# A decode block with cached attention: four load slots in the place of a used-up weight, a q projection on column tiles, and a new load order

## The chip, the core and the metric

The kernel runs on one core of a Trainium2 chip. The metric is the device time of one execution in microseconds (us); the median over several executions counts. The engines are PE (matrix products and weight loads), DVE (vector work), ACT (activations), POOL and SP; SP issues all loads here, in one fixed order.

## The reference

Two layers, each of attention over a cache and a gated FFN, for four batches of one new token. Both layers use the same weights and the same caches.

```python
def _A_ref(x, k_cache, v_cache, wq, wo):      # x [4,1,512], caches [4,8,8192,128]
    q = (x @ wq).reshape(B, Sq, 32, 128).transpose(0, 2, 1, 3)
    k = jnp.repeat(k_cache, 4, axis=1); v = jnp.repeat(v_cache, 4, axis=1)
    p = softmax(einsum("bhqd,bhkd->bhqk", q, k) * 128 ** -0.5)
    o = einsum("bhqk,bhkd->bhqd", p, v)
    return o.transpose(0, 2, 1, 3).reshape(B, Sq, 4096) @ wo
def _B_ref(x, w_gate, w_up, w_down):          # F = 1792
    return (silu(x @ w_gate) * (x @ w_up)) @ w_down
x = x + _A_ref(_layernorm(x), ...);  x = x + _B_ref(_layernorm(x), ...)   # twice
```

All is bfloat16. Each cache holds 67 MB, and the four batches are independent of each other.

## The kernel before

**Units.** The caches are read in units of 1 MB: one batch b, one KV head g (8 of them), and one half cp of the 8192 positions. That makes 16 K units and 16 V units for each batch and layer. SBUF has a pool of `NSLOT = 11` slots of 8 KB per partition for them; a unit takes a slot from its load until PE has used it.

**A layer of one batch.** Each K unit is transposed on DVE (L568, two halves) and multiplied with the spread-out q on PE (L580), into four PSUM banks. After 16 units comes a softmax (L598 to L670). Then each V unit is multiplied with the probabilities on PE: as a rule by `rows` (L720, 16 products of 256 columns on four column tiles per unit, after which DVE transposes, adds and scales, L739 to L743), and for the last three groups (`NLATE = 3`) by `columns` (L705, 32 products of four columns). A group is the two V units of one head; its sum stays in one PSUM bank from its first unit to its last. Three banks (4, 5, 6) are shared by all such sums, by the FFN, the q projection and the softmax's transposes. The output projection (L683) follows each group.

**The chain.** When the last layer-0 group of a batch is projected, `chain` runs: add to x, layer norm, FFN (gate and up L758, down L811), layer norm, and the q projection of layer 1 for all heads in two halves (`q_proj`, L460: 64 products of 128x128 weights with four columns in each half), then scale (L523), spread (L473) and copy into `qpad` (L533). Only then can the K units of layer 1 for this batch be multiplied. The stages of K units run in the order `KSEQ`: (layer 0, batch 0), (0,1), (1,0), (0,2), (1,1), (0,3), (1,2), (1,3).

**The order.** `ORDER` is one string of tokens, the order in which SP issues loads: `K` is the next K unit, `a` a V unit of layer 0 (a + batch, head, half), `b` a V unit of layer 1 that is loaded again, `c` a V unit of layer 1 that is not loaded again, because its slot was kept from layer 0, and the weights by name. A `c` token loads nothing; its place only gives a priority. The class `Plan` simulates engines, slots, banks and loads with fixed costs, and from that fixes every engine's order of work, each unit's slot and each sum's bank. At run time semaphores hold the dependencies (waits at L62, loads issued at L92), but the order on an engine does not change. `wq_sb` is 32 KB per partition, and its last use is the q projection of batch 3.

Of the kernel before, what the change touches and what calls it, by code (L numbers as in the profile page):

```python
# [102 lines left out]
class Step:  # L103
    __slots__ = ("eng", "us", "deps", "fn", "prio", "take", "free", "start", "end", "loads", "slot_of", "n")

    def __init__(self, eng, us, fn, deps, prio, take=None, free=None, n=0):
        self.n = n
        self.eng, self.us, self.fn, self.prio = eng, us, fn, prio
        self.deps = [d for d in deps if d is not None]
        self.take, self.free = take, free  # L110
        self.start = self.end = None
        self.slot_of = None


class Plan:
# [3 lines left out]
    PAGE_N = 256  # L119
    LOAD_LEAD = 1.8  # L120
    LOAD_TAIL = 1.7
# [19 lines left out]
    def run(self):  # L141
# [66 lines left out]
        while left:  # L208
# [37 lines left out]
            if s.slot_of is not None:  # L246
                slots.append((s.end + self.HOP, self.slot[s.slot_of]))
            left -= 1
            finish(s)
# [4 lines left out]
    def emit(self):  # L254
        for s in sorted(self.steps + self.loads, key=lambda s: (s.start, s.prio[0])):
            s.fn()


ORDER = ("K c241 c230 K x a061 c201 c021 c310 c240 K c110 c100 c101 c311 a021 K wq K c000 c020 wo3 c001 K K K "
         "K K c231 a060 c040 K c161 c160 K c330 K K c111 c041 K K a071 c301 K a041 K c200 wo0 a070 a050 a040 "  # L260
         "K K K K a010 a020 a051 a031 K c300 K K K a011 K K K wo1 K c331 K wu1 K a000 a001 a030 wo2 wg0 wg1 "
         "wd0 wu0 wd1 a140 a141 a130 a120 a131 K K K K K K K K K K K K K K K K K a121 a150 K a151 a170 K a160 "
         "K K K a161 K K K K K a110 a111 a171 K K a100 a101 b060 K K b061 K b010 b011 b030 b071 b031 b050 "
         "b070 b051 K K K K a250 K K K K K K K a210 K a251 K K K K K a211 a260 a270 K a271 a200 K K a240 K "
         "a231 a201 K K K K a220 a221 a230 K K K a241 K K K a261 b130 b131 K b120 b121 b140 b141 b171 b170 "
         "b150 b151 K a361 a360 K a370 K K K K K K K K a371 K K K K K K a320 a351 a350 a321 a340 a330 a310 "
         "a331 a300 a341 a311 a301 b271 K b270 b260 b210 b211 K b261 K K K K K K K K K K K K K K b221 b250 "
         "b220 b321 b251 b340 b341 b370 b371 b320 b350 b351 b360 b361 ")
NSLOT = 11
NP = 2  # L270
NQB = 1
NLATE = 3


def bass_interleave_layers__gqa_block_cached__swiglu_ffn__decode_kernel(
# [33 lines left out]
    with ExitStack() as es:  # L309
# [57 lines left out]
        prog = {n: sem(f"prog_{n}") for n in engines}  # L367
        sem_slot = [sem(f"sem_slot{i}") for i in range(NSLOT)]
        sem_x = sem("sem_x")
# [85 lines left out]
        def q_proj(heads, deps, tag):  # L455
            def mm():
                bk = pbk(tag)
                for h in heads:
                    for kt in range(KT):
                        op("pe", lambda e: e.matmul(ps[:, bk * BW + h * B:bk * BW + (h + 1) * B],  # L460
                                                    lhsT=wq_sb[:, kt, h * Dh:(h + 1) * Dh],
                                                    rhs=xnT[:, kt * B:(kt + 1) * B],
                                                    start=(kt == 0), stop=(kt == KT - 1)),
                           reads=["wq", "xnT"], writes=[f"pb{bk}"], sig=(kt == KT - 1 and h == heads[-1]))
            return PL.add("pe", 0.029 * KT * len(heads), mm, deps, CHAIN, take=tag, n=2 * KT * len(heads))

        def q_spread(src, n, key, deps, tag):
# [48 lines left out]
        def q_half(b, hf, mm_tag, deps, prior):  # L516
            nh = Hq // 2
            k = kpos[(1, b)] % NQB

            def scl():  # L520
                bk = pbk(mm_tag)
                src = ps[:, bass.ds(bk * BW + b + hf * nh * B, nh, step=B)]
                op("dve", lambda e: e.tensor_scalar(qT2[:, hf * nh:(hf + 1) * nh], src, qscale[:, b:b + 1], None,  # L523
                                                    op0=ALU.mult),
                   reads=[f"pb{bk}", "qscale"], writes=[f"qT2_{hf}"])
            s1 = PL.add("dve", 0.21, scl, deps, CHAIN, free=mm_tag)
            tag = f"qs{b}_{hf}"
            sp = q_spread(qT2[:, hf * nh:(hf + 1) * nh], nh, f"qT2_{hf}", [s1], tag)

            def cp():  # L530
                bk = pbk(tag)
                got = ps[:, bk * BW:bk * BW + NES * nh].rearrange("p (s g j) -> p s g j", s=NES, j=REP)
                op("dve", lambda e: e.tensor_copy(q_diag(k, hf * G // 2, G // 2), got),  # L533
                   reads=[f"pb{bk}"], writes=[f"qpad{k}_{hf}"])
            return PL.add("dve", 0.21, cp, [sp, prior], CHAIN, free=tag)
# [3 lines left out]
        def unit_ap(u, h):  # L539
            s = PL.slot[home[u]]  # L540
            return pool[:, s, h * UE:(h + 1) * UE], f"slot{s}_{h}"

        def load_pair(u):
            kind, l, b, g, cp = u

            def fn():
                s = PL.slot[home[u]]
                cache = A_k_cache if kind == "k" else A_v_cache
                src = cache[b, g, cp * 2 * CR:(cp + 1) * 2 * CR, :].rearrange("(p t) d -> p (t d)", p=P)
                T.dma("sp", pool[:, s, :], src, sem_slot[s], writes=[f"slot{s}_0", f"slot{s}_1"])  # L550
            home[u] = u
            return PL.load(2.515, fn, u)

# [6 lines left out]
        def k_pair(u, ld, prio, prev):  # L560
            _, l, b, g, cp = u
            qbuf = kpos[(l, b)] % NQB
            tr = []
            for h in range(2):
                def t(h=h):
# [6 lines left out]
            def qk():  # L572
                kt = [unit_ap(u, h) for h in range(2)]
                ap = [k[0].rearrange("p (t e j s) -> p t e j s", e=2, j=32, s=2) for k in kt]
                for es_ in range(NES):
                    for a in range(4):
                        rows = slice(32 * a, 32 * (a + 1))
                        for h in range(2):
# [3 lines left out]
                                                        rhs=ap[h][rows, :, es_ // 2, :, es_ % 2],  # L582
                                                        start=(g == 0 and es_ == 0),
                                                        stop=(g == G - 1 and es_ == NES - 1),
                                                        tile_position=(32 * a, 32 * c), skip_group_check=True),
                               reads=[f"qpad{qbuf}_{2 * g // G}", kt[h][1]], writes=[f"pb{a}"],
                               sig=(es_ == NES - 1 and a == 3 and h == 1))
            st = PL.add("pe", 1.95, qk, tr + [qd, prev] + (scores_free[0] or []), prio, n=64)
            st.slot_of = u
            return st  # L590
# [100 lines left out]
        def v_group(l, b, g, lds, prios):  # L691
# [4 lines left out]
            for i, cp in enumerate(VCP):  # L696
                u = ("v", l, b, g, cp)

                def columns(u=u, i=i, cp=cp):
                    bk = pbk(tag)  # L700
                    for h in range(2):
                        ap, key = unit_ap(u, h)
                        for t in range(NB):
# [5 lines left out]
                                                        stop=(i == NCP - 1 and h == 1 and t == NB - 1)),  # L709
                               reads=pt(q) + [key], writes=[f"pb{bk}"], sig=(h == 1 and t == NB - 1))  # L710

                def rows(u=u, i=i, cp=cp):
                    bk = pbk(tag)
                    for h in range(2):
                        ap, key = unit_ap(u, h)
                        v = ap.rearrange("p (t d) -> p t d", d=Dh)
                        for f in range(2):
                            col = p_col(2 * cp + h, g, 8 * f)
                            for n in range(4):
# [6 lines left out]
                                   reads=pt(q) + [key], writes=[f"pb{bk}"], sig=(h == 1 and f == 1 and n == 3))  # L726
                st = PL.add("pe", 1.0 if direct else 0.95, columns if direct else rows,
                            [prev, p_ready[(l, b)], lds.get(u)], prios[i], take=tag if i == 0 else None,
# [5 lines left out]
            def nm():  # L734
                bk = pbk(tag)
                got = ps[:, bk * BW:bk * BW + REP]
                if not direct:
# [7 lines left out]
                   reads=[f"pb{bk}", f"invL{q}", "osum"], writes=[f"oT{l}_{g}"])  # L745
            n = PL.add("dve", 0.17 if direct else 0.6, nm, [prev, inv_ready[(l, b)]], CHAIN, free=tag)
            if l == 0 or b == B - 1:
# [84 lines left out]
        def chain(b, deps, prior):  # L832
# [7 lines left out]
            for hf in range(2):  # L840
                tag = f"q{b}_{hf}"
                mm = q_proj(range(hf * Hq // 2, (hf + 1) * Hq // 2), [cen, mm], tag)
                out_.append(q_half(b, hf, tag, [mm, qs], prior))
            q_ready[(1, b)] = out_

        def w_piece(t_sb, src, key, us):
            return PL.load(us, lambda: T.dma("sp", t_sb, src, sem(f"sem_{key}"), writes=[key]), None)

# [11 lines left out]

        kseq = [("k", l, b, g, cp) for l, b in KSEQ for cp in range(NCP) for g in range(G)]
        VCP = list(range(NCP))
        tokens = ORDER.split()
        kept = {("v", 0) + tuple(int(x) for x in t[1:]) for t in tokens if t[0] == "c"}
        vgroups = [(l, b, g) for b in range(B) for l in range(2) for g in range(G)]
        late_groups = []
        for t in reversed(tokens):
            if t[0] == "b" and len(late_groups) < NLATE and (1, int(t[1]), int(t[2])) not in late_groups:
                late_groups.append((1, int(t[1]), int(t[2])))

# [5 lines left out]
        for npos, t in enumerate(tokens):  # L876
            if t == "K":
                u = kseq[ki]
                ki += 1
                loads[u] = load_pair(u)  # L880
                prio[u] = [npos]
            elif t[0] in "abc":
                u = ("v", int(t[0] != "a")) + tuple(int(x) for x in t[1:])
# [39 lines left out]
        def make_k(i):  # L923
# [6 lines left out]
            for n, u in enumerate(us_):  # L930
                st = k_pair(u, loads[u], prio[u], st)
            last_q[i] = st
# [42 lines left out]
        def fin2():  # L975
            bk = pbk("out")
            op("dve", lambda e: e.tensor_copy(xlast, bank_bf(bk)[0:B * NQ, 0:P]), reads=[f"pb{bk}"], writes=["xrow"])
        PL.add("dve", 0.15, fin2, [s], CHAIN, free="out")

# [36 lines left out]
```

## Time and profile before

| | |
|---|---|
| median of 3 runs | 642.69 us (642.42 to 643.32) |
| the profiled execution | 643.24 us, its span 641.5 us |
| moved on the load queue | 257.19 MB in 41048 packets |
| PE, DVE, ACT busy | 418.5, 421.6, 40.2 us |
| mean granted PE clock | 0.685 |
| K units, V units loaded | 128, 104 |
| median from issue to landing, K and V units | 9.6 and 10.7 us |

The span runs from the first to the last instruction. In the page's second part the span is cut into 40 equal slices of 16 us: PEclk is the PE clock granted in tenths of full speed (9 is 90% or more), DMA the mean busy share of the 16 DMA engines, GB/s what they moved. In the timeline a line is start, duration, engine, line of the kernel, operation, result and operands, shapes, and how many instructions were merged; in square brackets stands how long the engine was idle before it, and what ended that. "issue" there means that the engine waited for nothing that the profile shows. The chain of waits goes back from the last instruction to what released it, step by step, and is read in order of time.

### The profile page before, as it was taken

Reading aid. Unit: us, or ns where it says so; the run is one execution under the profiler, and the core shown is the slowest. Engines: PE = TensorE matmul, PEld = TensorE weight load, DVE = VectorE, ACT = ScalarE, POOL = GpSimd, SP = SyncE. Lnnn points to the kernel's source line nnn. Section 1 sums busy time; section 2 is a strip of 40 time slices with the busy share of each in tenths; the row PEclk is TensorE's granted clock in tenths of the full one; section 3 lists DMA queues with packets and bytes.
Section 4 is the critical chain, followed back from the end, with each engine's and each line's share of the span. In section 5 each row is a group of like instructions: output and inputs, shape, how many; then the busy total and the mean of one; then the engine's idle time right before and its main releaser. Section 6 shows DMA issues by size and latency. Waiting matters only on the chain.

```text
span 641.5 us, 18860 instructions
## 1 busy us (share of the span) xinstructions
PE 418.5 (65%) x8721; PEld 210.1 (33%) x8721; DVE 421.6 (66%) x740; ACT 40.2 (6%) x106; POOL 1.8 (0%) x8
## 2 busy tenths in 40 slices
PE   0276455656677676578775675777666776876765
PEld 0231131215532242235322242224522254622355
DVE  5278864745289979565686976576487763599722
ACT  1000200003000100000200100000200020000200
POOL 1000000000000000000000000000000000000000
PEclk9995676776576789766577686565676675578675
DMA  8999999999999999999999999999999999999991
GB/s 359 411 417 420 407 419 421 406 413 382 403 369 419 421 420 419 420 420 398 415 411 421 420 417 421 420 412 421 404 403 421 418 422 419 393 398 422 420 418 68
DMA packets 41127, 258.39 MB, mean 403 GB/s; under 512 B 3924, under 2 KB 9816, under 8 KB 10840
## 3 DMA queue, kind: packets, MB, share of 16 engines
q1 hardware_dynamic: 41048, 257.19, 97.8%
q8 instruction: 68, 1.11, 0.7%
q14 instruction: 11, 0.09, 0.0%
HBM read 257.17 MB, written 0.00 MB: 401 GB/s over the span
## 4 chain that ended last, share of the span: by engine, by line
DMA 60%; PE 18%; DVE 15%; SPq 4%; issue 2%; ACT 1%
DMA pool<-in_A_k_cache_dram 34%; DMA pool<-in_A_v_cache_dram 26%; DVE pool L568 8%; PE ps L580 7%; PE ps L720 5%; SPq L92 4%; DVE negm L598 2%; PE ps L460 1%; DVE ps L739 1%; PE ps L758 1%; DVE pp L627 1%; PE ps L638 1%; PE ps L683 1%; PE ps L811 1%; DVE osum L741 1%
## 5 line engine op out<-in xcount | busy, mean ns | idle before, releaser
L568 DVE STREAM_TRANSPOSE pool<-pool 128x1024 uint32<-128x1024 uint32 x256 | 303.4, 1223 | 69.0 <-DMA pool<-in_A_k_cache_dram 62.2
L580 PE MATMUL ps<-pool,qpad 32*32 32x512 bf16 x4096 | 229.4, 528 | 84.6 <-DVE pool L568 82.0
L580 PEld LDWEIGHTS ps<-pool,qpad 32*32 32x32 bf16 x4096 | 67.3, 107 | 220.6 <-DVE pool L568 155.0
L720 PE MATMUL ps<-pool,pp 128*32 128x256 bf16 x1952 | 98.2, 352 | 60.5 <-DMA pool<-in_A_v_cache_dram 47.3
L720 PEld LDWEIGHTS ps<-pool,pp 128*32 128x32 bf16 x1952 | 54.6, 116 | 100.5 <-DMA pool<-in_A_v_cache_dram 67.9
L739 DVE STREAM_TRANSPOSE ps<-ps 128x256 f32<-128x256 f32 x61 | 27.9, 457 | 68.9 <-PE ps L720 68.9
L602 ACT ACTIVATE pp<-ps,negm 128x512 bf16<-128x512 f32 x32 | 21.6, 685 | 336.4 <-DVE negm L598 249.2
L683 PE MATMUL ps<-oT,wo_sb 128*128 128x4 bf16 x640 | 22.8, 166 | 15.4 <-DVE oT L743 10.9
L460 PE MATMUL ps<-xnT,wq_sb 128*128 128x4 bf16 x640 | 18.4, 166 | 19.2 <-DMA wq_sb<-in_A_wq_dram 17.5
L683 PEld LDWEIGHTS ps<-oT,wo_sb 128*128 128x128 bf16 x640 | 20.2, 102 | 28.9 <-DVE oT L743 19.1
L598 DVE TENSOR_REDUCE negm<-ps 128x1 f32<-128x512 f32 x32 | 19.8, 679 | 13.0 <-PE ps L580 13.0
L460 PEld LDWEIGHTS ps<-xnT,wq_sb 128*128 128x128 bf16 x640 | 17.6, 103 | 21.0 <-DMA wq_sb<-in_A_wq_dram 17.6
L638 PE MATMUL ps<-ident,pp 128*128 128x128 bf16 x128 | 14.9, 293 | 9.5 <-DVE pp L627 8.8
L638 PEld LDWEIGHTS ps<-ident,pp 128*128 128x128 bf16 x128 | 11.9, 137 | 14.9 <-DVE pp L627 10.8
L446 ACT ACTIVATE lnv<-var,eps_sb 128x4 f32<-128x4 f32 x10 | 3.0, 297 | 219.3 <-DVE var L441 219.3
L741 DVE TENSOR_REDUCE osum<-ps 128x4 f32<-128x32 f32 x61 | 11.7, 191 | 2.1
L743 DVE TENSOR_TENSOR oT<-osum,invL 128x4 bf16<-128x4 f32 x61 | 10.3, 169 | 2.1
L705 PE MATMUL ps<-pp,pool 128*128 128x4 bf16 x192 | 5.9, 167 | 6.5 <-DMA pool<-in_A_v_cache_dram 6.5
L647 ACT ACTIVATE pp<-ps 128x1024 bf16<-128x1024 bf16 x8 | 8.2, 1024 | 23.9 <-PE ps L638 23.9
L627 DVE TENSOR_SCALAR pp<-pp,alpha 128x512 bf16<-128x512 bf16 x32 | 9.0, 343 | 1.1 <-ACT alpha L620 1.1
L758 PE MATMUL ps<-xnT,wg_sb 128*128 128x4 bf16 x280 | 8.2, 166 | 2.1 <-DVE xnT L435 1.5
L811 PE MATMUL ps<-hT,wd_sb 128*128 128x4 bf16 x280 | 8.5, 166 | 1.1 <-DVE hT L803 0.6
(61 smaller groups left out, 126.7 us busy)
## 6 DMA issues: line engine op xcount, KB each, us to landing
pool<-in_A_k_cache_dram SPq DMA_DIRECT2D x128, 1024.0 KB, 9.6
pool<-in_A_v_cache_dram SPq DMA_DIRECT2D x104, 1024.0 KB, 10.7
wq_sb<-in_A_wq_dram SPq DMA_DIRECT2D x1, 4096.0 KB, 24.0
wo_sb<-in_A_wo_dram SPq DMA_DIRECT2D x4, 1024.0 KB, 18.0
wu_sb<-in_B_w_up_dram SPq DMA_DIRECT2D x2, 896.0 KB, 13.9
wg_sb<-in_B_w_gate_dram SPq DMA_DIRECT2D x2, 896.0 KB, 15.9
wd_sb<-in_B_w_down_dram SPq DMA_DIRECT2D x2, 896.0 KB, 12.4
pp<-in_A_x_dram SPq DMA_DIRECT2D x1, 4.0 KB
```

Of the source, the lines that this page charges most:

```text
L92: ins = self.eng[engname].dma_start(out_ap, in_ap)
L460: op("pe", lambda e: e.matmul(ps[:, bk * BW + h * B:bk * BW + (h + 1) * B], lhsT=wq_sb[:, kt, h * Dh:(h + 1) * Dh], rhs=xnT[:, kt * B:(kt ...
L568: op("dve", lambda e: e.transpose(v, v), reads=[key], writes=[key])
L580: op("pe", lambda e: e.matmul(ps[32 * c:32 * (c + 1), a * BW:(a + 1) * BW], lhsT=qpad[rows, qbuf, es_, g, :], rhs=ap[h][rows, :, es_ // 2, ...
L598: op("dve", lambda e: e.tensor_reduce(negm[:, q, a:a + 1], bank(a), AX.X, ALU.max, negate=True), reads=[f"pb{a}"], writes=[f"negm{q}_{a}"])
L602: op("act", lambda e: e.activation(pblk(q)[:, :, a, :], bank(a).rearrange("p (t j) -> p t j", j=32), ACTF.Exp, bias=negm[:, q, a:a + 1], s ...
L627: op("dve", lambda e: e.tensor_scalar(seg, seg, alpha[:, q, a:a + 1], None, op0=ALU.mult), reads=[f"pp{q}_{a}", f"alpha{q}"], writes=[f"pp ...
L638: op("pe", lambda e: e.matmul(stg[:, t * P:(t + 1) * P], lhsT=pp[:, q, blk * P:(blk + 1) * P], rhs=ident[:], is_transpose=True, start=True ...
L683: op("pe", lambda e: e.matmul(ps[:, OPJ * BW + nq * B:OPJ * BW + (nq + 1) * B], lhsT=wo_sb[:, h, nq * P:(nq + 1) * P], rhs=oT[:, l, h, :], ...
L720: op("pe", lambda e: e.matmul(ps[32 * n:32 * (n + 1), bk * BW:bk * BW + 256], lhsT=pp[:, q, col:col + 32], rhs=v[:, 8 * f:8 * (f + 1), 32 ...
L739: op("dve", lambda e: e.transpose(blk, blk), reads=[f"pb{bk}"], writes=[f"pb{bk}"])
L741: op("dve", lambda e: e.tensor_reduce(osum[:], diag, AX.X, ALU.add), reads=[f"pb{bk}"], writes=["osum"])
```

## The change

- Four more slots: the place of `wq_sb` is divided into four slots, handed to the plan when PE has done the last q projection (`gives`). `load_pair` and `unit_ap` go through `slot_sb`.
- The q projection of layer 1 (`q_rows`) holds x on PE and streams wq: 16 products of 512 columns on four column tiles for each half, followed by a transpose of a whole bank on DVE. The first q projection (`q_first`) stays as it was.
- Group 6 of the last batch alone is multiplied by columns (`LATE`), not three groups. The very last V unit comes in two loads of half its size, and its products are split alike (`TAILSPLIT`).
- K units: layer 0 takes heads 4 to 7 ahead of heads 0 to 3, layer 1 the other way round; before, both went by half of the positions and then by head. Code to keep K units too is there, but off (`KM` is 0).
- A new `ORDER`, and new costs in the plan. Of `c` tokens there are 25 in place of 24, of `b` tokens 39 in place of 40; batch 3 keeps seven units where each batch kept six.

```diff
-    LOAD_LEAD = 1.8
+    LOAD_LEAD = 2.1
...
+            for i in range(s.gives):
+                slots.append((s.end + self.HOP, self.nslots + i))
...
-         "wd0 wu0 wd1 a140 a141 a130 a120 a131 K K K K K K K K K K K K K K K K K a121 a150 K a151 a170 K a160 "
...
-         "a331 a300 a341 a311 a301 b271 K b270 b260 b210 b211 K b261 K K K K K K K K K K K K K K b221 b250 "
-         "b220 b321 b251 b340 b341 b370 b371 b320 b350 b351 b360 b361 ")
+ORDER = ("c320 K c321 c041 c240 a061 wg0 K a071 c241 wo2 K x wq K c201 a051 a021 K c131 K c130 a031 c311 K K "
+         "c110 K c111 K K c120 c121 c051 c040 K K K K K wo0 K a020 K a030 wg1 K a060 wo3 K c261 a070 K c050 K "
+         "K K K c301 c260 K K K K K K a050 K a040 a041 a000 a001 wo1 a011 a010 c340 wd1 wu0 c341 wu1 wd0 a140 "
+         "a141 a160 a171 a170 a161 K K K K K c200 K K K K K K c300 K K K K K a100 a101 a150 a151 K K a130 K "
+         "a120 a121 K K K K K a111 K K K K K a110 K K a131 b000 b001 K b021 b030 b020 b070 b031 b071 b010 "
+         "b011 K K K a210 K K K K K K K K K K K K K a270 a271 K a220 a250 a221 K a211 K K a230 a240 K K K "
+         "b100 c060 K a200 a241 K c061 K a251 a231 K K K K a260 a201 a261 b150 K K b101 b161 b151 b170 b160 "
+         "b171 b140 b141 K a310 a350 K K K K K K K K K K a351 K K K K K a370 a361 a360 a371 a330 a301 a340 "
+         "a320 a341 a311 a300 a331 a321 b210 b211 b270 b271 b230 K K K K K K K K K K K K K K K K b221 b251 "
+         "b250 b220 b371 b370 b351 b310 b360 b231 b350 b330 b331 b361 ")
 NSLOT = 11
-NLATE = 3
+LATE = (6, )
+KM = (0, 0, 0, 0)
+TAILSPLIT = True
...
+        def q_rows(hf, deps, tag):
+            nh = Hq // 2
+            def mm():
+                bk = pbk(tag)
+                for kt in range(KT):
+                    w = wq_sb[:, kt, hf * nh * Dh:(hf + 1) * nh * Dh].rearrange("p (h d) -> p h d", d=Dh)
+                    for n in range(4):
+                        op("pe", lambda e: e.matmul(ps[32 * n:32 * n + B, bk * BW:(bk + 1) * BW],
+                                                    lhsT=xnT[:, kt * B:(kt + 1) * B],
+                                                    rhs=w[:, :, 32 * n:32 * (n + 1)],
+                                                    start=(kt == 0), stop=(kt == KT - 1), tile_position=(0, 32 * n)),
...
+                blk = bank(bk).bitcast(mybir.dt.uint32)
+                op("dve", lambda e: e.transpose(blk, blk), reads=[f"pb{bk}"], writes=[f"pb{bk}"])
+                src = ps[:, bass.ds(bk * BW + b, nh, step=32)]
...
-            s1 = PL.add("dve", 0.21, scl, deps, CHAIN, free=mm_tag)
+            s1 = PL.add("dve", 0.98, scl, deps, CHAIN, free=mm_tag)
...
+        def slot_sb(s):
+            return pool[:, s, :] if s < NSLOT else wq_sb[:, s - NSLOT, :]
...
-            return PL.load(2.515, fn, u)
+            if u != last_unit:
+                return PL.load(2.495, fn, u)
+            def half(h):
+                s = PL.slot[home[u]]
+                src = A_v_cache[b, g, cp * 2 * CR:(cp + 1) * 2 * CR, :].rearrange("(p h t) d -> p h (t d)", p=P, h=2)
+                T.dma("sp", slot_sb(s)[:, h * UE:(h + 1) * UE], src[:, h, :], sem_half if h == 0 else sem_slot[s],
...
+            return [PL.load(1.25, lambda: half(0), u), PL.load(1.25, lambda: half(1), None)]
...
+                if u == last_unit:
+                    lds[u], first = lds[u][1], lds[u][0]
+                    prev = PL.add("pe", 0.5, lambda columns=columns: columns(hs=(0,)),
+                                  [prev, p_ready[(l, b)], first], prios[i], take=tag if i == 0 else None, n=32)
+                    st = PL.add("pe", 0.5, lambda columns=columns: columns(hs=(1,)), [prev, lds[u]], prios[i], n=32)
...
-                st = PL.add("pe", 1.0 if direct else 0.95, columns if direct else rows,
+                st = PL.add("pe", 1.0 if direct else 1.02, columns if direct else rows,
...
-            n = PL.add("dve", 0.17 if direct else 0.6, nm, [prev, inv_ready[(l, b)]], CHAIN, free=tag)
+            n = PL.add("dve", 0.17 if direct else 0.88, nm, [prev, inv_ready[(l, b)]], CHAIN, free=tag)
...
-                mm = q_proj(range(hf * Hq // 2, (hf + 1) * Hq // 2), [cen, mm], tag)
+                mm = q_rows(hf, [cen, mm], tag)
                 out_.append(q_half(b, hf, tag, [mm, qs], prior))
+            if b == B - 1:
+                mm.gives = KT
...
-        kseq = [("k", l, b, g, cp) for l, b in KSEQ for cp in range(NCP) for g in range(G)]
+        k_order = [(g, cp) for cp in range(NCP) for g in range(G)]
+        k_order = [x for x in k_order if x[0] >= G // 2] + [x for x in k_order if x[0] < G // 2]
+        def k_units(l, b):
+            stay = k_order[len(k_order) - KM[b]:]
+            seq = k_order if l == 0 else stay + [x for x in k_order[len(k_order) // 2:] if x not in stay] + \
+                k_order[:len(k_order) // 2]
+            return [("k", l, b) + x for x in seq]
+        kseq = [u for l, b in KSEQ for u in k_units(l, b)]
...
-        late_groups = []
-        for t in reversed(tokens):
...
+        late_groups = [(1, B - 1, g) for g in LATE]
```

## The prediction

> **What bounds the kernel now.** I read the slices of the page first, then its DMA queues, then windows of four microseconds where the GB/s row sags, then the timeline inside the worst of them, then the end of the chain of waits.
>
> ```profile
> PEclk9995676776576789766577686565676675578675
> DMA  8999999999999999999999999999999999999991
> GB/s 359 411 417 420 407 419 421 406 413 382 403 369 419 421 420 419 420 420 398 415 411 421 420 417 421 420 412 421 404 403 421 418 422 419 393 398 422 420 418 68
> q1 hardware_dynamic: 41048, 257.19, 97.8%
> ```
>
> The DMA row is full from the second slice to the last but one, and the rate is flat at 420 to 421 GB/s wherever only 1 MB cache units move. 257.19 MB at 420.5 GB/s are 611.6 us of the 641.5 us span: this is a stream, and work on an engine counts only where it stops the stream or stands after it. The other 30 us are a head of about 2.75 us, a tail of about 13 us after the stream, and some 14 us of sag. Part of the sag is weight pieces in short packets (DMA share above 1.0 at a lower rate), which both kernels load alike. The rest is a stream that ran dry:
>
> ```profile
> 168.00:172.00 4.00, 2.97 (x84) 2.81 (x85) 1.49 (x9) 0.50 (x2) 0.00 (x0) 0.50 1.01 422
> 172.00:176.00 4.00, 2.29 (x83) 2.02 (x84) 0.46 (x2) 0.00 (x0) 0.00 (x0) 0.50 0.91 369
> 176.00:180.00 4.00, 2.63 (x57) 1.64 (x60) 2.72 (x6) 0.00 (x0) 0.00 (x0) 0.50 0.52 178
> 544.00:548.00 4.00, 3.91 (x111) 3.25 (x108) 3.21 (x11) 0.25 (x1) 0.00 (x0) 0.50 0.96 385
> 548.00:552.00 4.00, 3.55 (x72) 2.36 (x68) 1.23 (x8) 0.17 (x1) 0.00 (x0) 0.50 0.93 367
> 552.00:556.00 4.00, 3.96 (x123) 3.37 (x120) 1.23 (x5) 0.33 (x2) 0.00 (x0) 0.50 1.01 397
> ```
>
> The last three columns are granted clock, DMA share, GB/s. Against 421, 172 to 180 us lost 4 x (52 + 243) / 421 = 2.8 us (2.3 us by the share) and 544 to 556 us lost 4 x (36 + 54 + 24) / 421 = 1.1 us. Both lie under a serial chain (last output projection, FFN, layer norm, q projection) that must end before the next 16 K units can be used, while the slots fill with them. Batch 0's chain in the timeline:
>
> ```profile
> 169.74 1.86 PE L460 MATMUL ps<-xnT,wq_sb 128*128 128x4 bf16 x64
> 171.93 1.87 PE L460 MATMUL ps<-xnT,wq_sb 128*128 128x4 bf16 x64 [0.33 <-DVE qT L523]
> 176.03 0.26 PE L473 MATMUL ps<-qT,ident 128*32 128x16 bf16 x13 [1.06 <-issue]
> 176.63 1.90 PE L720 MATMUL ps<-pool,pp 128*32 128x256 bf16 x32 [0.34 <-DVE qpad L533]
> 181.02 5.67 PE L580 MATMUL ps<-pool,qpad 32*32 32x512 bf16 x97
> ```
>
> Each half of q takes 1.87 us at clock 0.50, PE stands 1.06 us with nothing to wait for but its own instructions, and V work lies between q and the first K product.
>
> **The change part by part.**
>
> One load less. Before keeps 24 V units of layer 0 for layer 1 (c tokens) and loads 40 b units; after keeps 25 and loads 39. A unit is 1024 KB: 1.0486 MB / 0.4205 = 2.5 us. Nothing hides a byte of a full stream. -2.5.
>
> The new order at batch 0's chain. Its FFN needs the last weight piece. Before, five V units (12.5 us) follow that piece until the first K of (1,0); after, six (15.0 us), the last piece standing at the same place in the stream within half a unit. The last layer-0 unit now comes 4.8 us later (two weight pieces fewer ahead of the FFN's), landing near 152.6 instead of 147.8; with 2.7 us of product, evacuation and projection the norm could start near 156, and in before it stood behind a softmax until 156.61 anyway. So the chain ends as before and its cover grows by 2.5 us, against an idle of 2.3 to 2.8. Late next could be V work that PE runs after q, as at 176.63, so I take -1.8 (from -2.5 to +1.5). Moving x and wq behind wg0 and wo2 puts the first q about 2.5 us later; the slots not yet taken then are six, 15 us of loads, against some 6 us from wq's landing to the first freed K slot, so nothing runs dry: 0 (up to +1).
>
> The q projection on column tiles. Before, 64 weight loads and 64 products of four columns per half. After, 16 products of 512 columns on four column tiles. The nearest row is the V product in rows (L720, also 128*32, 16 at a time):
>
> ```profile
> 614.18 0.62 PE L720 MATMUL ps<-pool,pp 128*32 128x256 bf16 x16 [0.24 <-DMA pool<-in_A_v_cache_dram]
> 558.92 1.04 PE L720 MATMUL ps<-pool,pp 128*32 128x256 bf16 x16 [1.90 <-DMA pool<-in_A_v_cache_dram]
> ```
>
> The first is at full clock, the second at 0.50. Halving the clock added 0.42 us, so 0.42 us is streaming and 0.20 us fixed. With twice the columns a half of q takes 0.20 + 0.84 = 1.04 us at full clock and 0.20 + 1.68 = 1.88 us at 0.50. The chains run at 0.50, so PE gains nothing there. Against this stands the Trainium skill, "TensorE: Matmul & The Clock Gate", Part 3: three column tiles of 512 columns gave 2.38 times, not 3 times. Four at that efficiency give 3.17 times; by the page's cold gap (N / 1.2 ns) 16 products are 16 x 427 / 3.17 = 2.15 us, an estimate that would lengthen a chain by 2 x 0.3 us. I take the row of this trace: 0.
>
> Behind each half stands a new DVE transpose of 128x512 in PSUM. L739 does 128x256 in 457 ns and L568 128x1024 in 1223 ns, so about 1 ns an element: 0.71 us, eight times. PE has the second half of q queued behind the first, so the first transpose lies beside it; the second is off the first K product's path, because layer 1 now takes all eight K units of groups 0 to 3 first, which need only half 0. Uncovered it would be +0.7 us per chain. What is surely gone is 96 PE instructions per half; the 1.06 us of "issue" above is where that could show. Together: a chain ends 0 to 2 us earlier, or 1 us later if the transposes are not covered. It pays only where the stream is dry, counted below.
>
> The last chain. Here seven kept units leave four of 11 slots rotating, not five, until the four slots in wq's place come free at the end of the last q product. In before the units ahead of a301 landed at 532.96 and 535.45, so it landed at 537.9; the last q product (554.77 + 2.04) ended at 556.8, 18.9 us later. I take 17 to 19 us for after. In that time the stream is fed by b210 b211 b270 b271 b230 and four K units: 9 x 2.5 = 22.5 us, counted from the end of a321's data, some 1.9 us ahead of its landing, so 20.6 us behind it. The first issue of the program is at 0.74 us and data run from about 2.75, so a slot that comes free gives data 2.0 us later: 19 to 21 us, dry for 0 to 0.4 us. But the 1.1 us lost in before came earlier, while V units held slots behind chain work on PE, and one slot fewer makes that worse by up to a unit: I take 1.5 us dry, net +0.4 (from -1.1 to +4). The load into wq's place waits on SP for PE's last q product, with all later loads behind it: K units, which would wait anyway. After that, eight slots turn instead of five in the last K stage, which already ran at 416 to 426 GB/s with five: 0.
>
> The other two chains, 286 to 305 and 435 to 460 us, cost about 1 us of dry stream now; same cover, 30 us and more: 0 (-0.6 to +1.5).
>
> The tail.
>
> ```profile
> 610.92 19.43 DMA pool<-in_A_v_cache_dram
> 630.35 0.05 issue
> 630.39 1.03 PE ps L705 x32
> 631.44 0.18 DVE oT L743
> 631.67 0.60 PE ps L683 x16
> ```
>
> The last unit lands at 630.35 and then waits for its own 32 products. In two loads of half the size, the first half's 16 products run while the second lands, and about half of 1.03 us goes; groups 2 and 5 change from columns (two units, about 2 us) to rows plus transposes (1.3 to 2.1 us and 0.9 us of DVE), but land 2.5 us or more ahead of the end, and only group 6 is last in both. -0.45. The rule against this is in the Trainium skill, "DMA: Bandwidth & Descriptors", Rules for kernel authors: at least 1 MiB per DMA, with some 2.0 us fixed for each. If that were paid twice in series, this step would cost +1.5. But 1 MB loads here follow each other every 2.5 us, which at 420 GB/s is their bytes alone, so a queued load's fixed part is covered by the one ahead of it. I keep -0.45, with +0.5 as upper end.
>
> The plan's constants (LOAD_LEAD, 2.495, 1.02, 0.88, 0.21) and the sixteen K steps' order have no cost of their own; they and the new ORDER set who waits for whom in PE's fixed order. Unknown elsewhere: 0, from -1 to +2.
>
> Sum for the profiled execution: 643.24 (span 641.5 and 1.74 around it) - 2.5 - 1.8 + 0.4 - 0.45 = 638.9. That execution stood 0.55 above the median of the runs shown, 642.69, so the median of after should be 638.3.
>
> **The rivals.** *Bytes only.* The new order moves the dry places without shrinking them: -2.5 - 0.45, or 639.7. For it: the idle at 176 us came from PE's order meeting a late q, and a new order can do it again elsewhere.
>
> *The last chain starves.* In group (1,2,3), b230 comes at the head of the last chain and b231 sixteen K units later, so its sum holds one of the three shared PSUM banks (4, 5, 6) for some 60 us. The FFN wants gate and two up halves at once, q two banks, and the V fillers one. If a chain step then stands in PE's fixed order for a bank, everything behind it stands too, and with four slots rotating each microsecond beyond the cover is one of dry stream. The cover is used up already, so 4 to 5 us more of chain brings the kernel to no change, and 6 to 8 us give 644 to 646. Against it: the FFN's first bank is free 0.2 us after gate ends, beside the first up half, and before also had a group open there (b260 and b261 around two K units) and lost only 1.1 us.
>
> *The column tiles do not overlap.* By the same row a product of 512 columns streams 0.42 us at clock 0.50; 16 in series are 6.7 us instead of 1.88, each chain grows by some 10 us, the first and last without cover: near 655. The row excludes it: its 16 in series would have taken 1.7 us, not 0.62.
>
> *The wq slots do nothing*, because they come too late. Then four slots turn at 2.0 + 2.5 + 1.9 us of load and 4.4 us of transposes and products, 2.7 us per K unit against 2.5: +0.2 on twelve units, +2.4, or 640.7; with a late chain on top it ends inside 0.2% of before.
>
> **How the numbers follow.** The summed case 0.57, its own range 636.3 to 640.7; bytes only 0.18; slots of no use 0.10 (half of it inside 0.2%); starving 0.14; tiles in series 0.01. What a measurement of this kernel can tell from no change is about 0.2%, 1.3 us, so faster means below 641.4 and slower above 644.0. Faster: 0.57 + 0.18 + 0.05 = 0.80. Of the starving case some 0.04 lies within 0.2% and 0.10 above; so same 0.09, slower 0.11. Range 635.8 to 642.0: it leaves out most of the starving case and a little at the fast end.
>
> **What would show it.** 39 late V units and 256.1 MB on q1; at 172 to 180 us a DMA share above 0.9; at about 545 to 560 us a dip of 1 to 3 us worth of data; q products of 1.0 to 2.1 us per 16 and eight transposes of 0.7 us; the last landing followed by 16 columns of 0.5 us; a span near 637. Wrong: a share below 0.8 in any window of four microseconds after 10 us other than the last chain's, or more than 3 us dry there, and above all a stream below 418 GB/s where only cache units move.

## The result, and the profile after

The changed kernel takes 639.55 us (median of 4 runs, 638.97 to 639.93), beside 642.83 us for the kernel before (4 runs). The ratio is 0.9948 with a 95% interval of 0.9931 to 0.9965, so 3.3 us less, from 2.2 to 4.4. The profiled execution took 639.93 us with a span of 638.1 us. The prediction was 638.3 us, in a range of 635.8 to 642.0.

The slices and the load queue of the changed kernel, to be read against those of before:

```profile
PEclk9997668685556667676676777575766675578685
DMA  8999999999989999999999999999999999999992
GB/s 349 416 421 420 408 404 421 418 410 390 412 347 417 423 419 419 422 418 408 407 398 421 422 417 420 422 419 412 416 405 420 416 420 421 393 420 420 421 416 85
q1 hardware_dynamic: 41048, 256.14, 97.7%
```

One unit fewer went over the queue (257.19 to 256.14 MB). The rate is flat at 420 to 421 GB/s as before, and the sag did not shrink. Adding up (421 - rate) x 4 us / 421 over all windows of four microseconds up to 624 us gives 14.1 us before and 14.1 us after. Only its places changed:

| stretch, us | before | after |
|---|---|---|
| 0 to 172 (head, weight pieces) | 5.8 | 5.9 |
| 172 to 184 (chain of batch 0) | 2.8 | 3.3 |
| 284 to 332 (chain of batch 1) | 1.4 | 2.0 |
| 420 to 480 (chain of batch 2) | 1.7 | 1.2 |
| 540 to 572 (last chain) | 1.9 | 1.1 |
| the rest | 0.4 | 0.7 |

The two windows at batch 0's chain, where a DMA share above 0.9 had been forecast. A line is the window, its length, the busy us of PE, PE's weight loads, DVE, ACT and POOL with their instructions, then clock, DMA share and GB/s. Line numbers are those of the kernel that is shown:

```profile
172.00:176.00 4.00, 2.09 (x32) 0.57 (x32) 1.67 (x4) 0.00 (x0) 0.00 (x0) 0.50 0.91 369
176.00:180.00 4.00, 2.30 (x64) 1.36 (x56) 1.38 (x6) 0.00 (x0) 0.00 (x0) 0.50 0.45 145
```

The end of the chain of waits:

```profile
608.25 18.87 DMA pool<-in_A_v_cache_dram
627.16 0.59 PE ps L743 x16
627.75 0.87 PE ps L721 x32
```

The last landing, at 627.12 us, is followed by 16 products that take 0.59 us together, in place of 32 that took 1.03 us. From the landing to the end it is 11.0 us, and was 11.15 us. The landing itself came 3.23 us earlier, 2.5 us of it the unit.

### The profile page after: what moved, and what is told of

Its sections match the earlier page's. It is cut to its first block, busy times and chain, and to the rows that moved or that the text cites. A ratio compares the mean times of both kernels' runs of the same rounds, so it can differ in the third digit from the quotient of the medians.

```text
span 638.1 us, 17970 instructions
## 1 busy us (share of the span) xinstructions
PE 420.7 (66%) x8273; PEld 198.9 (31%) x8273; DVE 428.0 (67%) x752; ACT 40.2 (6%) x106; POOL 1.8 (0%) x8
## 3 DMA queue, kind: packets, MB, share of 16 engines
q1 hardware_dynamic: 41048, 256.14, 97.7%
q8 instruction: 65, 1.06, 0.7%
## 4 chain that ended last, share of the span: by engine, by line
DMA 66%; DVE 15%; PE 15%; SPq 2%; issue 2%; ACT 0%
DMA pool<-in_A_k_cache_dram 37%; DMA pool<-in_A_v_cache_dram 24%; DVE pool L605 10%; PE ps L617 5%; PE ps L758 4%; DMA wo_sb<-in_A_wo_dram 3%; DMA wq_sb<-in_A_k_cache_dram 2%; SPq L92 2%; PE ps L481 1%; PE ps L804 1%; DVE negm L636 1%; PE ps L676 1%; DVE ps L544 1%; DVE ps L785 1%; DVE wq_sb L605 1%
## 5 line engine op out<-in xcount | busy, mean ns | idle before, releaser
L605 DVE STREAM_TRANSPOSE pool<-pool 128x1024 uint32<-128x1024 uint32 x240 | 284.2, 1222 | 72.8 <-DMA pool<-in_A_k_cache_dram 66.6
L617 PE MATMUL ps<-pool,qpad 32*32 32x512 bf16 x3840 | 222.0, 542 | 75.7 <-DVE pool L605 75.1
L758 PE MATMUL ps<-pool,pp 128*32 128x256 bf16 x1952 | 99.8, 358 | 61.1 <-DMA pool<-in_A_v_cache_dram 44.9
L617 PEld LDWEIGHTS ps<-pool,qpad 32*32 32x32 bf16 x3840 | 63.9, 109 | 210.6 <-DVE pool L605 149.9
L758 PEld LDWEIGHTS ps<-pool,pp 128*32 128x32 bf16 x1952 | 56.1, 120 | 101.6 <-DMA pool<-in_A_v_cache_dram 62.6
L676 PE MATMUL ps<-ident,pp 128*128 128x128 bf16 x128 | 14.2, 285 | 9.1 <-DVE pp L665 8.3
L605 DVE STREAM_TRANSPOSE wq_sb<-wq_sb 128x1024 uint32<-128x1024 uint32 x16 | 18.6, 1212 | 0.5 <-DMA wq_sb<-in_A_k_cache_dram 0.2
L617 PE MATMUL ps<-wq_sb,qpad 32*32 32x512 bf16 x256 | 12.6, 409 | 7.1 <-DVE wq_sb L605 6.9
L481 PE MATMUL ps<-wq_sb,xnT 128*4 128x512 bf16 x128 | 13.9, 589 | 1.9 <-DVE qT L546 1.4
L544 DVE STREAM_TRANSPOSE ps<-ps 128x512 uint32<-128x512 uint32 x8 | 5.8, 725 | 7.8 <-PE ps L481 7.8
L804 PE MATMUL ps<-xnT,wu_sb 128*128 128x4 bf16 x280 | 8.6, 166 | 2.0 <-DVE gs L824 1.5
```

The lines of the kernel that those rows point to most:

```text
L481: op("pe", lambda e: e.matmul(ps[32 * n:32 * n + B, bk * BW:(bk + 1) * BW], lhsT=xnT[:, kt * B:(kt + 1) * B], rhs=w[:, :, 32 * n:32 * (n + ...
L544: op("dve", lambda e: e.transpose(blk, blk), reads=[f"pb{bk}"], writes=[f"pb{bk}"])
L605: op("dve", lambda e: e.transpose(v, v), reads=[key], writes=[key])
L617: op("pe", lambda e: e.matmul(ps[32 * c:32 * (c + 1), a * BW:(a + 1) * BW], lhsT=qpad[rows, qbuf, es_, g, :], rhs=ap[h][rows, :, es_ // 2, ...
L676: op("pe", lambda e: e.matmul(stg[:, t * P:(t + 1) * P], lhsT=pp[:, q, blk * P:(blk + 1) * P], rhs=ident[:], is_transpose=True, start=True ...
L758: op("pe", lambda e: e.matmul(ps[32 * n:32 * (n + 1), bk * BW:bk * BW + 256], lhsT=pp[:, q, col:col + 32], rhs=v[:, 8 * f:8 * (f + 1), 32 ...
```

## Experiments

Times are medians, and differences are those of the medians unless a profile is named; the sag by stretch is worked out as above, from one profiled execution of each kernel.

**1. Spreads that wait.** The changed plan's banks show something that the prediction had missed. `make_qpad1` spreads q for batches 1, 2 and 3 of layer 0 as soon as q is there. The sum stays in its PSUM bank until `qpad` is free, since there is one `qpad`. In the plan two of the three shared banks are held in this way to 224 and 359 us. In the trace of the changed kernel the spreads of all four batches run together at 36 us (16 products each), and the sums of batches 2 and 3 are copied out 190 and 324 us later:

```profile
35.89 1.03 PE L494 MATMUL ps<-qT,ident 128*32 128x32 bf16 x64 [1.49 <-DVE qT L531]
227.03 0.28 DVE L518 CAST qpad<-ps 128x128 bf16<-128x128 f32 x1
360.42 0.28 DVE L518 CAST qpad<-ps 128x128 bf16<-128x128 f32 x1
```

The kernel before does the same, with copies at 223.57 and 365.56 us. So batch 0's chain runs on a single bank. Its timeline in the changed kernel:

```profile
169.81 1.88 PE L481 MATMUL ps<-wq_sb,xnT 128*4 128x512 bf16 x16
171.74 0.73 DVE L544 STREAM_TRANSPOSE ps<-ps 128x512 uint32<-128x512 uint32 x1 [0.94 <-PE ps L481]
172.79 1.88 PE L481 MATMUL ps<-wq_sb,xnT 128*4 128x512 bf16 x16 [1.11 <-DVE qT L546]
177.06 1.90 PE L758 MATMUL ps<-pool,pp 128*32 128x256 bf16 x32 [0.35 <-DVE qpad L556]
```

The second half of q waits 1.11 us for DVE to transpose and scale the first, because both use one bank. The V units stand behind all of it, with their slots, until 177.06. Even the layer norm's sum stands behind two V units: it starts at 168.68 us, when DVE has emptied their bank.

```diff
-            sp = q_spread(qT1[:, bass.ds(b, Hq, step=B)], Hq, "qT1", [dep], tag)
+            sp = q_spread(qT1[:, bass.ds(b, Hq, step=B)], Hq, "qT1", [dep, prior], tag)
```

> The changed kernel, with the spread of q for layer 0 of batches 1 to 3 made to wait in the plan for the stage that frees qpad, not run at 36 us. Theory: those early spreads hold two of the three shared PSUM banks until 224 and 359 us, so the chain of batch 0 runs on one bank (q halves one after the other, V units behind them) and the stream runs dry at 172 to 184 us for 3.3 us. Then this kernel loses under 1 us there and takes 636.5 to 637.5 us. Rival: the dry place comes from too few slots (six kept units); then the 3.3 us stay and the time is 639.5 us.

Measured: 637.43 us, ratio to before 0.9915 (0.9902 to 0.9927), an interval that lies clear of the changed kernel's. The spread of batch 2 now runs at 222.89 us, that of batch 3 at 357.27 us. The windows and the chain of this kernel:

```profile
172.00:176.00 4.00, 2.38 (x48) 1.55 (x48) 0.10 (x1) 0.00 (x0) 0.00 (x0) 0.73 1.01 414
176.00:180.00 4.00, 2.22 (x52) 1.47 (x48) 2.53 (x7) 0.00 (x0) 0.00 (x0) 0.50 1.00 406
```

```profile
166.36 3.63 PE L481 MATMUL ps<-wq_sb,xnT 128*4 128x512 bf16 x32
168.34 0.73 DVE L544 STREAM_TRANSPOSE ps<-ps 128x512 uint32<-128x512 uint32 x1 [1.26 <-PE ps L481]
169.93 0.83 PE L758 MATMUL ps<-pool,pp 128*32 128x256 bf16 x16
```

The norm's sum starts 3.7 us earlier, at 164.97 us; the two halves run back to back, the transpose lies beside the second, V work starts at 169.93, and the sag at 172 to 184 us is 0.2 us in place of 3.3. The number of slots and of kept units was the same, so banks made this place dry, not slots; the eighth experiment shows it in the kernel before as well. Of these 3.1 us, 2.1 came through, since the other stretches together lost about 1.1 us more. This kernel beats both.

**2. One kept unit fewer.**

```diff
- ... c311 ...   b351 b310 b360 ...
+ ...            b351 b310 b311 b360 ...
```

> The changed kernel with one kept V unit fewer (c311 is loaded again behind b310, 40 loads of V in layer 1 in place of 39). Theory: a byte of a full stream has a price, 2.5 us, so 642.0 us. Rival (the gain came from slots and the q projection, and a unit more fits into the sag): 640 us or less.

Measured: 642.97 us, so 3.4 us more than the changed kernel; its profiled execution (641.68) is 1.75 us above that of the changed kernel. The rival, that the unit would be hidden, falls. But the edit changes more than the bytes: batch 3 keeps six units, so five slots turn during the last chain, and the sag at 540 to 572 us is 0.1 us in place of 1.1. Less than 2.5 us in the profile fits that. Why the median lies higher is open: the profiled execution was the fastest of twelve, which spread up to 644.84 us.

**3. The old q projection in the new plan.**

```diff
-                mm = q_rows(hf, [cen, mm], tag)
+                mm = q_proj(range(hf * Hq // 2, (hf + 1) * Hq // 2), [cen, mm], tag)
... (scl without the transpose of the bank, cost 0.21)
```

> The changed kernel with the old q projection of layer 1 (64 products of four columns in each half, no DVE transpose of the bank, and the old costs in the plan). Theory: the column tiles bring nothing where the stream is dry, because a half takes 1.88 us either way and the transposes stand between the halves on the one free bank: 639.0 to 640.5 us, up or down with how the plan's order falls. Rival: the new projection is what shortened the chains; then 641 us or more.

Measured: 642.85 us, 3.3 us more, with twelve executions from 641.15 to 644.67 us. The rival's figure was met: without the column tiles this order is not faster than before. At batch 0's chain the theory was right, though: there the old form loses less (2.4 us of sag against 3.3). More was lost in the chains of batches 1 and 2 (284 to 332 us: 3.0 us of sag against 2.0; 420 to 480: 2.9 against 1.2). The window where the dip of batch 2's chain begins, first in this kernel, then in the changed one:

```profile
460.00:464.00 4.00, 1.17 (x15) 0.24 (x17) 3.40 (x7) 2.97 (x9) 0.00 (x0) 0.50 0.91 309
```

```profile
460.00:464.00 4.00, 1.87 (x28) 0.57 (x32) 3.63 (x9) 1.48 (x5) 0.00 (x0) 0.65 1.01 418
```

The V units of this chain were used up at 460.32 us, in the changed kernel at 458.46. Two things in the traces make up such a delay. First, the second half of q took 1.87 us here; in the changed kernel the clock had risen by then, and it took 1.03 us:

```profile
454.50 1.03 PE L481 MATMUL ps<-wq_sb,xnT 128*4 128x512 bf16 x16
```

Second, PE stopped for 0.77 us in the middle of a V unit's products, with "issue" as the reason. With the old form, 96 more PE instructions per half, such stops of 0.6 us or more stand right behind q in the chains of all of the first three batches (0.71, 1.17 and 0.77 us here; 1.06, 0.62 and 1.96 us in the kernel before), and at none of these places in the changed kernel. The two were not separated.

A longer wait that also reads "issue" comes later, and it is something else:

```profile
468.25 1.25 DVE L603 STREAM_TRANSPOSE pool<-pool 128x1024 uint32<-128x1024 uint32 x1 [2.99 <-DMA pool<-in_A_k_cache_dram]
469.66 0.63 DVE L685 COPY pp<-ps 128x1024 bf16<-128x1024 bf16 x1
470.39 1.90 PE L756 MATMUL ps<-pool,pp 128*32 128x256 bf16 x32 [2.54 <-issue]
```

The V products at 470.39 need the softmax's copy, which ends 0.10 us before them, and here the plan has put the transpose of a K unit ahead of that copy on DVE. In the changed kernel the copy comes first, and the V products start at 467.65 us, again 0.10 us behind it. So the new costs changed the plan's order too, and that is a third cause that this experiment does not take apart from the first two.

**4. The last unit in one load.**

```diff
-TAILSPLIT = True
+TAILSPLIT = False
```

> The changed kernel with the last V unit in one load. Theory: splitting gains 0.4 us of products and some of the stream's drain (from the last full microsecond to the last landing, 2.4 us before, 1.75 us after): 640.0 to 640.6 us. Rival (two half loads cost a fixed part more): 639.0 us or less.

Measured: 640.73 us, 1.2 us more, but the ratio's interval (0.9956 to 0.9977) overlaps that of the changed kernel, and the profiled execution was 0.3 us below it (639.6). In the chain of waits the 16 products are 32 again:

```profile
626.71 1.01 PE ps L743 x32
```

So the 0.42 us of products is shown in the traces. What the split does to the landing isn't: this kernel's came at 626.66 us, 0.46 earlier than with two loads. That the fixed part of a second load costs time finds no support in the medians.

**5. The slots of wq not given.**

```diff
-                mm.gives = KT
+                mm.gives = 0
```

> The changed kernel, but the four slots in the place of wq are never given to the plan (seven kept units, four of 11 slots turning through the last K stage). Theory, as in the prediction: four slots give a K unit every 2.7 us in place of 2.5, so some 2.4 us more, 642.0 us, with the loss spread over 560 to 600 us. Rival (the slots are what carries the gain): 645 us or more. Second rival (they bring nothing): 639.5 us.

Measured: 649.26 us, 9.7 us more. The first rival was right. A stretch with four slots turning, and one turn of a slot in the chain of waits (from the issue of a load at 587.31 us to the next at 599.50):

```profile
560.00:584.00 24.00, 17.54 (x280) 4.95 (x287) 20.39 (x18) 0.00 (x0) 0.00 (x0) 0.57 0.97 356
```

```profile
587.31 7.74 DMA pool<-in_A_k_cache_dram
595.07 2.38 DVE pool L605 x2
597.49 1.95 PE ps L617 x28
599.50 7.58 DMA pool<-in_A_v_cache_dram
```

The changed kernel has 422 GB/s there. A slot's turn is 12.2 us and not the 10.8 that the prediction added up: transposes and products take the 4.4 us that it had, but a load takes 7.7 us from issue to landing and not 6.4. The loss is not that of twelve units either: the sag from 540 to 624 us is 13.2 us against 1.4 (in an execution 2.0 us above the median). The four slots are what lets the last batch keep seven units.

**6. The two halves of one group together.**

```diff
- ... b271 b230 K ...        b310 b360 b231 b350 ...
+ ... b271 b230 b231 K ...   b310 b360 b350 ...
```

> The changed kernel with b231 loaded right behind b230, so that the bank of group (1,2,3) is not held through the last K stage. Theory: the last chain isn't short of banks; nothing gained: 639.5 to 641 us, and the last chain's dry place (1.1 us) about as before or smaller by the one V unit more of cover. Rival (the starving case of the prediction): the bank costs time there, and this takes 638.5 us or less.

Measured: 640.23 us (ratio 0.9953, 0.9941 to 0.9965), the same as the changed kernel; the last chain's sag is 1.0 us against 1.1. The starving case of the prediction is refuted: the bank that is held through the last K stage costs nothing that can be measured.

**7. The order of before in the new code.**

```diff
-ORDER = ("c320 K c321 c041 ...
+ORDER = ("K c241 c230 K x ...
...
+        op("dve", lambda e: e.memset(ps[:, 4 * BW:7 * BW], 0.0), writes=["pb4", "pb5", "pb6"])
```

> The changed kernel's code (column tiles, wq slots, one group by columns, split tail, new costs and K order) with the load order of before (24 kept units); the three shared PSUM banks are set to zero once at the start, on an idle DVE. Theory (the order pays only through its one load less, and the code through a shorter end and shorter chains): 641.5 to 642.5 us. Rival (the new order as such is worse, or better, by over 2 us): outside of that.

Measured: 642.77 us, ratio 1.0001 (0.9993 to 1.001), just outside the first theory's 641.5 to 642.5, on the side of no gain. Batch 0's chain is drier than in either kernel (4.1 us of sag at 172 to 184 us). Against the kernel before, the transpose between the halves on the one bank fits that: the halves start 2.98 us apart, 2.19 before. The three later chains together have 3.9 us against 5.1 before, so the two cancel, and the shorter end does not come through in the median.

This kernel and the changed one differ by the order alone, the zeroed banks aside: 3.2 us, with 1.05 MB more on the queue (2.5 us) and the same sag in all (14.2 and 14.1 us). That is the clearest sight of the price of a load. Neither the code without the order (642.77) nor the order without the column tiles (642.85) is faster than before. Together they bring 3.3 us.

**8. Spreads that wait, in the kernel before.** The edit is that of the first experiment.

> The kernel before, with only the spread of q for layer 0 made to wait for the stage that frees qpad. Theory: two banks held to 224 and 359 us cause the dry place of 172 to 180 us there too; its 2.8 us fall under 1 us and the time is 640 to 641 us, unless the changed order of work opens another dry place. Rival (slots cause it): 642.8 us with the dry place as before.

Measured: 644.37 us, ratio 1.0024 (1.0013 to 1.0034), slower. The sag at 172 to 184 us falls from 2.8 to 0.5 us, as the theory says. But a new one opens in batch 1's chain (284 to 332 us: 3.8 us against 1.4). The plan, with banks free, has put q there earlier, at 293.17 us where it began at 300.10, and PE stops within it:

```profile
293.17 3.28 PE L460 MATMUL ps<-xnT,wq_sb 128*128 128x4 bf16 x117
298.58 0.43 PE L460 MATMUL ps<-xnT,wq_sb 128*128 128x4 bf16 x11 [2.14 <-issue]
299.47 3.59 PE L720 MATMUL ps<-pool,pp 128*32 128x256 bf16 x64
```

PE stands for 2.14 us in the middle of the old q projection, waiting for nothing that the profile shows. Four V units with their slots stand behind it, and the stream falls to 201 GB/s at 300 to 304 us. In the first experiment, with 16 products in place of 64, the same release of the banks opened no such place (0.8 us of sag there). That the number of products makes the stop was not tested alone.

## Why the prediction held, step by step

The forecast for the profiled execution was -4.35 us, and -3.31 us was measured. The measured sum is -2.5 for the unit, 0.0 for the sag (forecast: -1.4), about -0.65 for the end of the stream (not forecast) and -0.17 behind the last landing.

- **One load less, -2.5:** shown. The queue moved 1.05 MB less, and with equal sag the stream is 2.5 us shorter. The seventh experiment, with one load more and equal sag, lost 3.2 us.
- **Batch 0's chain, -1.8:** wrong. It measured +0.5. The prediction's own signs of being wrong came here: a DMA share of 0.45, where one below 0.8 was such a sign, and 3.3 us dry, where more than 3 was. The chain kept its time and one more V unit lay in front of it, as forecast, but the step took cover against the chain's end as the limit. V work could not run beside the chain, since both had one bank; cover by more V units is then no cover. The first experiment shows it: with the banks free the sag there fell to 0.2 us, and the time by 2.1 us.
- **The q projection, 0:** its row was right (1.88 us per half at clock 0.50 and 1.03 us at 1.00, for 1.88 and 1.04 worked out), and the transposes measured 0.73 us for the 0.71 forecast. Two parts failed. On batch 0's one bank the transposes are not covered (172.79 - 169.81 = 2.98 us from half to half, against 2.19 before, so +0.8 where the bound was +0.7); the issue wait of 1.06 us is gone, and q is complete at about the same time (177.01 against 176.58). And "the chains run at 0.50, so PE gains nothing there" did not hold in batch 2's chain, where the clock rose within q; without the column tiles this order loses 3.3 us, by causes that the third experiment does not take apart. The estimate of 2.15 us from the Trainium skill's page "TensorE: Matmul & The Clock Gate" (Part 3, with the cold gap of Part 2) was not seen (1.88 us); the trace's row decided rightly.
- **The last chain, +0.4:** the forecast was 1.5 us dry and 1.2 us was measured between 548 and 560 us, so net +0.1. That one slot fewer makes this place dry fits the second experiment (five slots, 0.1 us). Better still, the dip at 560 to 568 us of before (0.9 us) is gone; without the slots of wq it is 2.0 us in the fifth experiment.
- **The tail, -0.45:** 0.42 us of products. The forecast's sum from that landing to the end was not reached, as the write of the result took 0.24 us more in this execution. The stream's drain was 0.65 us shorter (from where the stream at its full rate would end, to the last landing: 2.4 us before, 1.75 after); its cause is open, since the fourth experiment's profile has no longer one. The Trainium skill's page "DMA: Bandwidth & Descriptors" states the 2.0 us that the prediction weighed in "Anatomy of one DMA — SWDGE (gpsimd) path", for loads that GpSimd issues, while SP issues them here; a loss by the second load was not seen.
- **The rivals:** "bytes only", 639.7, is what the time came to (639.55), and nearly for its reason: the sag moved and did not shrink. The prediction gave it 0.18. The starving case was tested and fell. The slots' price was put at +2.4 and is +9.7.

So the direction and the range held, and one step of 1.8 us did not. That the time still came within 1.3 us of the number is in part luck: the shorter drain, which the prediction had not counted, made good some of the missing gain.

## What to carry to other kernels

When a stream is full, first count its bytes; then, for each place where it runs dry, ask which resource the waiting work lacks, and not only how much work lies in front. Here it was PSUM banks, two of three, each held for 190 us and more by a sum of 0.3 us, because the sum was computed as soon as it could be and not when its reader was ready. A change of order and a change of an operation can each be worth nothing and together 3.3 us, so undo them one at a time in both directions. And where a plan is made anew for every variant, look for what else moved before a difference is put down to the edit.

## What the runs showed of the hardware that was not expected

- PE stood still in the middle of runs of products with "issue" as the only reason: 2.14 us within 128 products of 128x128 weights with four columns (eighth experiment), 1.96 us behind q of batch 2 in the kernel before. Such stops stood behind the old form of q in three chains and at none of these places in the changed kernel, with a quarter of the products. But the column tiles do not end them: one of 1.92 us stood at 530 us in the seventh experiment. What PE lacked there is not shown. And not every "issue" is such a stop: the 2.54 us at 470.39 us ended 0.10 us after the DVE copy that the products need.
- The granted clock in the chains was mostly 0.50, and the same 16 products of q took 1.88 us and, where it had risen, 1.03 us. It did not simply follow the form of the products: in the changed kernel both halves of q ran at 0.50 for batches 0 and 1, and in the first experiment q of batch 2 took 1.92 and 1.79 us. What raised it is open.
